# More buffers for the attention units of the first 256 queries, their loads of q and k without the wait for a v, row blocks of layer 1 one step apart, and a new plan

## The chip, the cores and the metric

The kernel runs on one core of a Trainium2 chip. The metric is device time in microseconds (us) from launch to end; of each kernel the median of its runs counts. The core has five instruction queues that matter here: TensorE (PE, matmuls, with its weight loads PEld), VectorE (DVE), ScalarE (ACT), GpSimd (POOL, all but unused) and SyncE (SP, which issues every DMA transfer).

## What is computed

Block-causal attention, an expert layer with softplus, and a second one with SoLU and a normalisation:

```python
# q, k, v: B=4, H=8, S=576, D=64
scores = q @ k.T / sqrt(64)
scores = where(query // 64 >= key // 64, scores, -1e9)
attn = exp(scores - max) / (sum + 1e-9)
x = (attn @ v)                       # -> 2304 tokens x 512
g = log1p(exp(-abs(x @ w_in))) + maximum(x @ w_in, 0)       # 512 -> 2048
x = g @ w_out                                               # 2048 -> 512
h = x @ w_in2                                               # 512 -> 1024
solu = h * softmax(h)
out = ((solu - mean) / sqrt(var + 1e-6) * g_ln) @ w_out2    # 1024 -> 512
```

## The kernel before

**The plan.** The body issues no instruction at once. It adds tasks (a step with its engine, a duration and the tasks it needs) to a `Plan`, whose `run` is a list scheduler: it takes, engine by engine, the ready task of the lowest rank, and writes the instructions out in the order found. A rank is the task's own number plus `RANK[group]` (a base and a slope per member of the group) plus `OFF[step]`. Each engine then works through its own queue strictly in that order. So two tables of numbers set the order on every engine, and a queue whose next instruction has to wait holds up all that stand behind it.

**Attention, first part.** `UnitA` is one of 16 units: one batch element (4) and one pair of heads (4), for the first 256 queries, in fp32. Its steps: SP loads q and k in one tile `qkA` (L515, three buffers) and v in `vA` (L519, two buffers); PE makes the scores with 4 matmuls (`mm_qk`, L204; 8 records in the trace); DVE masks (L538), takes maxima (L543) and scales them (L546); ACT takes exp (L552) into `eA`, one of two fixed tiles; DVE makes reciprocals (L556, L559) and multiplies `eA` by them (`norm`, L564, four instructions); PE transposes `eA` (L571, six); ACT or DVE copies that out of the accumulator into `psA` (one buffer; helper lines L210 on ACT, L212 on DVE); PE multiplies by v (`pv`); ACT or DVE writes the high half of x (L586) and DVE the low half (L590) into `xt`. A unit has its accumulator in the bank R, r, acc or hp. Units 0 to 3 are row block 0 (a row block is 256 tokens), units 4 to 7 row block 1, and so on. `UnitC`, later, does the other 320 queries.

The two loads of a unit depend on each other and on older units so:

```python
self.t_qk = add("SP", ..., self.load_qk, [opened] + g(p1, "t_v") + g(at_of(prev, n - 3), "t_mqk"), DMA_LAT)
self.t_v = add("SP", ..., self.load_v, [opened, self.t_qk] + g(p2, "t_pv"), DMA_LAT)
```

`p1` and `p2` are the unit one and two before; `g(u, "t_v")` is that unit's load of v.

**Weights.** A `Piece` is one 512 KB tile of weights that comes as 64-bit floats and is turned into a high and a low half: SP loads `raw` (L269, three buffers), ACT takes the absolute value (L274), DVE joins bits in three steps (L277, L280, L284, on `a`), ACT or DVE copies the high half, DVE subtracts for the low half (L294). There are 32 such pieces for layer 1, 16 `w1` (w_0 to w_15) and 16 `w2`.

**Layer 1.** A `Pair` is one row block and two of the 16 slices of 128 features: `a` (2 x 24 matmuls with w1 into `hp`, half a pair being 12 here), ACT abs, exp and ln (L647, L650, L653), DVE `stt` (L656), a copy to `gh`, DVE `gl` (L664), then `b` (2 x 12 matmuls with w2 into `acc` for row block 0 and `R` for row block 1). A half pair is thus 12 matmuls of `a` or of `b`. `SEQ` says in which order the pairs come. For the first two row blocks, whose weights are being converted, row block 1 follows row block 0 with the distance `LAG`:

```python
SEQ = [(0, p) for p in range(LAG)]
for p in range(8):
    SEQ += [(1, p)] + ([(0, p + LAG)] if p + LAG < 8 else [])
```

Pair n's `stt` must be done before pair n + 2 writes the same `hp`, and `b` runs in the order of the pairs. Layer 2 (`Tok`, 18 blocks of 128 tokens, with weights `U1` and `U2`) comes last. Four stretches of the span are used below: up to 155 us units, conversions and the first sixteen pairs; to 480 us the later units and row blocks; to 610 us the last row blocks and layer 2's weights; then layer 2.

Of the kernel before, what the change touches and what calls it, by code (L numbers as in the profile page):

```python
# [10 lines left out]
F32 = mybir.dt.float32  # L11
# [10 lines left out]
    "Pair.a": -160.87, "Pair.b": -32.19, "Pair.do_gh": -103.91, "Piece.bits0": 139.36, "Piece.do_lo@P": -201.40,  # L22
    "Piece.do_lo_g": 267.76, "Tok.a": 141.06, "Tok.x_hi": -460.68, "UnitA.x_hi": 408.37, "Tok.tr": -394.45,
    "Tok.bm": 359.77, "UnitC.pv": 348.22, "UnitC.tr": -288.31, "Pair.stt": -191.35, "Pair.do_gl": -445.21,
    "UnitC.qk_lo": -290.12,
}
RANK = {
# [3 lines left out]
    "Tok": (4285.47, -27.327),  # L31
# [163 lines left out]
def body(ctx: ExitStack, tc: tile.TileContext, qk, qkA, vP, vA, w1, w2, u1, u2, gln, out):  # L195
    nc = tc.nc
    PE, ACT, DVE, POOL, SP = nc.tensor, nc.scalar, nc.vector, nc.gpsimd, nc.sync
    plan = Plan()
    XTB, LAG = 3, 2
# [279 lines left out]
    class UnitA:  # L479
# [6 lines left out]
        def plan(self, prev, rank, opened):  # L486
# [11 lines left out]
            self.t_qk = add("SP", dma_ns(262144), rank - 2, self.load_qk, [opened] + g(p1, "t_v") + g(at_of(prev, n - 3), "t_mqk"), DMA_LAT)  # L498
            self.t_v = add("SP", dma_ns(131072), rank - 2, self.load_v, [opened, self.t_qk] + g(p2, "t_pv"), DMA_LAT)
            self.t_mqk = add("PE", 760, rank, self.mm_qk, [self.t_qk] + free)  # L500
            t = chain("DVE", rank, ((200, self.mask), (330, partial(self.max, 0)), (600, partial(self.max, 1)), (70, self.scale)), [self.t_mqk])
            t = add("ACT", 1580, rank, self.exp, [t] + g(p2, "t_tr"))
            t = chain("DVE", rank, ((72, self.den0), (90, self.den1), (918, self.norm)), [t])
            self.t_tr = add("PE", 650, rank, self.tr, [t])
            self.t_cp = add({"ACT": 708, "DVE": 870}, None, rank, self.copy, [self.t_tr] + g(p1, "t_pv"))
# [11 lines left out]
        def load_v(self):  # L517
            self.v = self.t([128, 2, 2, D], "vA")
            SP.dma_start(out=self.v, in_=vA[self.b, self.pr])  # L519

        def mm_qk(self):
# [7 lines left out]
            self.m, self.den = self.t([128, 2, 2], "mA"), self.t([128, 2, 2], "dA")  # L529
# [18 lines left out]
        def exp(self):  # L548
            self.e = state["eA"][self.n % 2]
# [23 lines left out]
        def copy(self, e):  # L573
            self.ps = self.t([128, 2, 384], "psA", 1)
            w = 2 // len(self.st)
            for j, st in enumerate(self.st):
                copy(e, self.ps[:, w * j:w * j + w], st[:, :, 0:384])
# [111 lines left out]
    def open_a():  # L689
# [5 lines left out]
        state["eA"] = [state["pat"].tile([128, 2, 384], F32, name=f"eA{n}") for n in range(2)]  # L695
# [328 lines left out]
```

## Time and profile before

| quantity | value |
|---|---|
| time, median of 3 runs | 810.62 us |
| the runs | 810.79, 810.62, 808.69 us |
| the profiled execution, its own time | 811.79 us |
| span of the profiled execution, first to last instruction | 810.0 us |
| mean granted clock of TensorE in it (1.00 is 2.4 GHz) | 0.989 |
| PE busy | 783.8 us (97%) |
| PEld busy | 694.7 us (86%) |
| DVE busy | 568.3 us (70%) |
| ACT busy | 394.0 us (49%) |
| POOL busy | 0.7 us |

A busy time is the sum of an engine's instructions in the span; PEld overlaps PE. A share is an average over the whole span, so it tells little of a stage; a view of busy time by stretches, views of one engine's waits, and timelines of single instructions stand further down. In a timeline a bracket at the end of a row is idle time just before it, and the instruction whose end closed that idle time.

### The profile page before, as it was taken

To read this page: it belongs to the slowest core of one execution; us is meant where nothing else is said; L and a number is where in the kernel's file an instruction comes from. 1 tells how busy PE (TensorE), PEld (TensorE's weight loads), DVE (VectorE), ACT (ScalarE), POOL (GpSimd) and SP (SyncE) were. 2 spreads that over 40 slices of the span, in tenths; PEclk is the share of its full clock that TensorE was granted. 3 is DMA by queue.
4 is the path that set the end of the run, shared out by engine and by line. 5 is a ranking of instruction groups with operands and counts; after the bars stand their busy time and mean duration, and the time that the engine had idled before them with its cause. 6 is when DMAs were issued, how large, how long until landed. Compare 5 with 4: busy or idle time off the path is not lost.

```text
span 810.0 us, 14410 instructions
## 1 busy us (share of the span) xinstructions
PE 783.8 (97%) x5752; PEld 694.7 (86%) x5752; DVE 568.3 (70%) x1291; ACT 394.0 (49%) x877; POOL 0.7 (0%) x6
## 2 busy tenths in 40 slices
PE   5689999999999999999999999999999999999998
PEld 3478989999888888888888889999898888888887
DVE  6989998565777667667776763768968486766661
ACT  5567776454565455555555553555633232322231
POOL 0000000000000000000000000000000000000000
PEclk9799999999999999999999999999999999999999
DMA  5636542202021112112112200227201111110001
GB/s 179 205 123 190 180 149 77 92 11 79 26 83 41 47 61 67 42 41 68 42 42 57 68 27 27 80 81 249 74 32 43 54 41 42 52 40 27 27 26 53
DMA packets 31203, 59.64 MB, mean 74 GB/s; under 512 B 2849, under 2 KB 14369, under 8 KB 31137
## 3 DMA queue, kind: packets, MB, share of 16 engines
q1 hardware_dynamic: 31136, 58.74, 22.9%
q8 instruction: 45, 0.74, 0.4%
q14 instruction: 22, 0.17, 0.1%
HBM read 49.29 MB, written 9.44 MB: 72 GB/s over the span
## 4 chain that ended last, share of the span: by engine, by line
PE 81%; DVE 8%; DMA 6%; ACT 3%; issue 1%; SPq 0%; ACTq 0%; DVEq 0%
PE hp L204 20%; PE acc L204 18%; PE op L204 12%; PE h L204 11%; PE S L204 5%; PE O L204 5%; PE T L452 4%; DMA raw_u<-in_u_dram 2%; DMA raw<-in_w_dram 2%; PE R L204 2%; PE tp L920 2%; PE r L204 1%; DVE a L284 1%; DVE eA L564 1%; DVE a L280 1%
## 5 line engine op out<-in xcount | busy, mean ns | idle before, releaser
L204 PE MATMUL hp<-xt,w 128*128 128x256 f32 x1728 | 221.6, 284 | 3.7 <-DVE t L656 3.4
L204 PEld LDWEIGHTS hp<-xt,w 128*128 128x128 f32 x1728 | 206.8, 189 | 9.5 <-DVE t L656 5.5
L204 PE MATMUL acc<-gh,w 128*128 128x256 f32 x768 | 148.1, 284 | 0.0
L204 PEld LDWEIGHTS acc<-gh,w 128*128 128x128 f32 x768 | 122.3, 189 | 0.7 <-issue 0.7
L204 PE MATMUL acc<-gl,w 128*128 128x256 f32 x384 | 107.3, 280 | 0.6 <-DVE gl L664 0.6
L204 PE MATMUL op<-w,w2w 128*128 128x512 f32 (+1 forms) x456 | 102.3, 382 | 0.0
L204 PE MATMUL h<-u,w 128*128 128x512 f32 x432 | 101.0, 391 | 0.0
L204 PEld LDWEIGHTS h<-u,w 128*128 128x128 f32 x432 | 80.6, 188 | 16.4
L204 PEld LDWEIGHTS op<-w,w2w 128*128 128x128 f32 x456 | 81.5, 188 | 15.3
L432 ACT ACTIVATE eC<-S,mC 128x384 f32<-128x384 f32 (+2 forms) x80 | 51.8, 649 | 46.4 <-DVE mC L421 46.4
L204 PEld LDWEIGHTS acc<-gl,w 128*128 128x128 f32 x384 | 72.5, 189 | 0.9 <-DVE gl L664 0.8
L656 DVE SCALAR_TENSOR_TENSOR t<-hp,t 128x512 f32<-128x512 f32 x72 | 49.4, 686 | 24.8 <-ACT t L653 24.2
L210 ACT ACTIVATE ps<-T 128x512 f32<-128x512 f32 (+1 forms) x74 | 40.8, 551 | 51.7 <-PE T L452 50.1
L647 ACT ACTIVATE t<-hp 128x512 f32<-128x512 f32 x72 | 42.8, 594 | 34.8 <-DVE gl L664 19.4
L664 DVE TENSOR_TENSOR gl<-t,gh 128x512 fp32r<-128x512 f32 x72 | 49.6, 690 | 3.8 <-ACT gh L210 2.4
L204 PE MATMUL acc<-gh,w2w 128*128 128x256 f32 x256 | 49.8, 285 | 0.0
L417 DVE TENSOR_REDUCE mC<-S 128x2 f32<-128x768 f32 (+2 forms) x48 | 46.9, 976 | 1.5 <-PE S L204 0.4
L650 ACT ACTIVATE t<-t 128x512 f32<-128x512 f32 x72 | 45.5, 633 | 1.8
L653 ACT ACTIVATE t<-t 128x512 f32<-128x512 f32 x72 | 45.2, 628 | 1.3
L452 PE MATMUL T<-ident,eC 128*128 128x128 f32 x288 | 45.3, 275 | 0.0
L872 ACT ACTIVATE e<-h,mx 128x1024 f32<-128x1024 f32 x18 | 20.1, 1116 | 50.5 <-PE tp L920 48.6
L926 ACT ACTIVATE w2w<-tp 128x512 fp32r<-128x512 f32 x36 | 20.7, 596 | 46.2 <-PE op L204 41.4
(156 smaller groups left out, 1128.6 us busy)
## 6 DMA issues: line engine op xcount, KB each, us to landing
raw<-in_w_dram SPq DMA_DIRECT2D x32, 512.0 KB, 4.0
qkC<-in_qk_dram SPq DMA_DIRECT2D x16, 480.0 KB, 3.4
raw_u<-in_u_dram SPq DMA_DIRECT2D x11, 512.0 KB, 3.6
v<-in_vP_dram SPq DMA_DIRECT2D x16, 320.0 KB, 2.9
x2s<-stg SPq DMA_DIRECT2D x18, 256.0 KB, 2.1
xr<-x2s SPq DMA_DIRECT2D x18, 256.0 KB, 3.2
qkA<-in_qkA_dram SPq DMA_DIRECT2D x16, 256.0 KB, 3.4
out_dram<-ob SPq DMA_DIRECT2D x15, 256.0 KB, 2.0
```

What stands on the lines that cost most here:

```text
L204: PE.matmul(out, lhsT, rhs, start=start, stop=stop, skip_group_check=True)
L210: ACT.activation(out, a, AF.Copy)
L417: DVE.tensor_reduce(out=self.m[:, 0:n], in_=self.scores(i), axis=AX.X if i < 2 else AX.XY, op=ALU.max, negate=True)
L432: ACT.activation(e, sc, AF.Exp, scale=0.125, bias=m[:, j:j + 1], accum_out=den[:, j:j + 1])
L452: PE.transpose(T[:, 128 * k:128 * k + 128], e[:, 128 * k:128 * k + 128], ident)
L647: ACT.activation(self.t, self.hp, AF.Abs)
L650: ACT.activation(self.t, self.t, AF.Exp, scale=-1.0)
L653: ACT.activation(self.t, self.t, AF.Ln, bias=1.0)
L656: DVE.scalar_tensor_tensor(out=self.t, in0=self.hp, scalar=0.0, in1=self.t, op0=ALU.max, op1=ALU.add)
L664: DVE.tensor_sub(self.gl, self.t, self.gh)
L872: ACT.activation(self.e, self.hh, AF.Exp, bias=self.mx, accum_out=self.ss)
L926: ACT.activation(self.lh[:, 4 * g:4 * g + 4, :], self.tp[g], AF.Copy)
```

## The change

Five edits and a new plan. `load_qk` of a unit needs the load of q and k before it, no longer the load of v before it. `vA`, `mA` and `dA` have four buffers in place of two, `psA` two in place of one, and `eA` is one of four tiles in place of two; the dependencies follow (a v needs the p*v of the unit four before, an exp the transposes of the unit four before, a copy the p*v two before). `LAG` is 1 in place of 2. The tables `OFF` and `RANK` have new numbers, and six steps that had no offset have one. The scratch space for dynamic DMA is set to 4096. Row numbers in the changed kernel are one or two higher.

```diff
 OFF = {
-    "Pair.a": -160.87, "Pair.b": -32.19, "Pair.do_gh": -103.91, "Piece.bits0": 139.36, "Piece.do_lo@P": -201.40,
...
+    "Pair.a": -75.59, "Pair.b": 18.34, "Pair.do_gh": 35.44, "Piece.bits0": 156.91, "Piece.do_lo@P": -117.94,
...
 RANK = {
-    "first": (278.93, 20.397), "A0": (636.85, 83.080), "A1": (-4008.02, 57.487), "A2": (-200.66, 24.018),
...
+    "first": (278.93, 20.397), "A0": (-2733.73, 86.246), "A1": (-2328.74, -30.508), "A2": (-843.36, 31.422),
...
-    XTB, LAG = 3, 2
+    XTB, LAG = 3, 1
...
-            self.t_qk = add("SP", dma_ns(262144), rank - 2, self.load_qk, [opened] + g(p1, "t_v") + g(at_of(prev, n - 3), "t_mqk"), DMA_LAT)
-            self.t_v = add("SP", dma_ns(131072), rank - 2, self.load_v, [opened, self.t_qk] + g(p2, "t_pv"), DMA_LAT)
+            p4 = at_of(prev, n - 4)
+            self.t_qk = add("SP", dma_ns(262144), rank - 2, self.load_qk, [opened] + g(p1, "t_qk") + g(at_of(prev, n - 3), "t_mqk"), DMA_LAT)
+            self.t_v = add("SP", dma_ns(131072), rank - 1, self.load_v, [opened, self.t_qk] + g(p1, "t_v") + g(p4, "t_pv"), DMA_LAT)
...
-            t = add("ACT", 1580, rank, self.exp, [t] + g(p2, "t_tr"))
+            t = add("ACT", 1580, rank, self.exp, [t] + g(p4, "t_tr"))
...
-            self.t_cp = add({"ACT": 708, "DVE": 870}, None, rank, self.copy, [self.t_tr] + g(p1, "t_pv"))
+            self.t_cp = add({"ACT": 708, "DVE": 870}, None, rank, self.copy, [self.t_tr] + g(p2, "t_pv"))
...
-            self.v = self.t([128, 2, 2, D], "vA")
+            self.v = self.t([128, 2, 2, D], "vA", 4)
...
-            self.m, self.den = self.t([128, 2, 2], "mA"), self.t([128, 2, 2], "dA")
+            self.m, self.den = self.t([128, 2, 2], "mA", 4), self.t([128, 2, 2], "dA", 4)
...
-            self.e = state["eA"][self.n % 2]
+            self.e = state["eA"][self.n % 4]
...
-            self.ps = self.t([128, 2, 384], "psA", 1)
+            self.ps = self.t([128, 2, 384], "psA", 2)
...
-        state["eA"] = [state["pat"].tile([128, 2, 384], F32, name=f"eA{n}") for n in range(2)]
+        state["eA"] = [state["pat"].tile([128, 2, 384], F32, name=f"eA{n}") for n in range(4)]
...
-    nc = _bacc.Bacc("TRN2", target_bir_lowering=False, num_devices=1)
+    nc = _bacc.Bacc("TRN2", target_bir_lowering=False, num_devices=1, dynamic_dma_scratch_size=4096)
```

The order moves on every engine. Three places follow, of before and then of the changed kernel.

The DMA queue (SP) at the start of the program, before; the numbers name the buffers, and the qkA loads are those of units 0 to 3 in order:

```order
L515 DMA qkA_136<-in_qkA_dram 128x512
L519 DMA vA_138<-in_vA_dram 128x256
L515 DMA qkA_140<-in_qkA_dram 128x512
L519 DMA vA_142<-in_vA_dram 128x256
L515 DMA qkA_144<-in_qkA_dram 128x512
L269 DMA raw_152<-in_w1_dram 128x1024
L269 DMA raw_162<-in_w1_dram 128x1024
L269 DMA raw_179<-in_w2_dram 128x1024
L519 DMA vA_237<-in_vA_dram 128x256
L515 DMA qkA_245<-in_qkA_dram 128x512
L269 DMA raw_253<-in_w1_dram 128x1024
```

The q and k of unit 3 (qkA_245) stand behind three weight pieces and the v of unit 2.

The same queue in the changed kernel:

```order
L517 DMA qkA_138<-in_qkA_dram 128x512
L521 DMA vA_140<-in_vA_dram 128x256
L517 DMA qkA_142<-in_qkA_dram 128x512
L521 DMA vA_144<-in_vA_dram 128x256
L517 DMA qkA_146<-in_qkA_dram 128x512
L521 DMA vA_154<-in_vA_dram 128x256
L270 DMA raw_156<-in_w1_dram 128x1024
L517 DMA qkA_167<-in_qkA_dram 128x512
L521 DMA vA_182<-in_vA_dram 128x256
L517 DMA qkA_185<-in_qkA_dram 128x512
L517 DMA qkA_190<-in_qkA_dram 128x512
L270 DMA raw_197<-in_w1_dram 128x1024
```

Unit 3's q and k (qkA_167) now stand behind one weight piece; the second weight piece has moved behind the q and k of unit 5, and four loads of v stand in front of it.

DVE, from the normalisation of unit 1 on (it multiplies eA_131), before:

```order
L564 TENSOR_SCALAR eA_131<-eA_131,dA 128x128 x2
L564 TENSOR_SCALAR eA_131<-eA_131,dA 128x256 x2
L277 TENSOR_SCALAR a<-a 128x512 x2
L280 SCALAR_TENSOR_TENSOR a<-raw,a 128x512 x2
L284 SCALAR_TENSOR_TENSOR a<-raw,a 128x512 x2
L556 TENSOR_SCALAR dA<-dA 128x4
L212 CAST xt<-R 128x256
L559 RECIPROCAL dA<-dA 128x4
L212 CAST w_0_81<-a 128x512
L590 TENSOR_TENSOR xt<-R,xt 128x256
L564 TENSOR_SCALAR eA_130<-eA_130,dA 128x128 x2
L564 TENSOR_SCALAR eA_130<-eA_130,dA 128x256 x2
```

Two weight pieces and the x of unit 0 stand between the normalisations of units 1 and 2 (unit 2 uses eA_130 again).

The same place in the changed kernel:

```order
L566 TENSOR_SCALAR eA_131<-eA_131,dA 128x128 x2
L566 TENSOR_SCALAR eA_131<-eA_131,dA 128x256 x2
L558 TENSOR_SCALAR dA<-dA 128x4
L545 TENSOR_REDUCE mA<-hp_114 128x1
L545 TENSOR_REDUCE mA<-hp_115 128x1
L561 RECIPROCAL dA<-dA 128x4
L278 TENSOR_SCALAR a<-a 128x512
L548 TENSOR_SCALAR mA<-mA 128x4
L566 TENSOR_SCALAR eA_132<-eA_132,dA 128x128 x2
L566 TENSOR_SCALAR eA_132<-eA_132,dA 128x256 x2
```

Unit 2's normalisation (eA_132, a tile of its own) comes six instructions behind unit 1's, and unit 3's maxima (hp) stand among them; the first weight piece has one of its three steps there.

PE behind the first `b` (w_0_97 and w_1_98 are the first two w2 tiles, acc belongs to row block 0), before:

```order
L204 MATMUL acc<-gh,w_1_98 128x256
L571 MATMUL r<-ident,eA_130 128x128 x6
L204 MATMUL r<-psA,vA 64x256 x2
L204 MATMUL r<-psA,vA 64x128 x2
L571 MATMUL R<-ident,eA_131 128x128 x6
L204 MATMUL acc<-gh,w_2_99 128x256
```

Behind the last matmul of the first b stand the transposes and p*v of unit 6 and the transposes of unit 7, then the second b of row block 0.

The same place in the changed kernel:

```order
L205 MATMUL acc<-gh,w_1_98 128x256
L205 MATMUL hp_115<-xt,w_0_81 128x256 x12
L205 MATMUL hp_115<-xt,w_1_82 128x256 x12
L205 MATMUL hp_114<-xt,w_2_83 128x256 x12
L205 MATMUL hp_114<-xt,w_3_84 128x256 x12
L205 MATMUL r<-qkA 128x128 x2
L205 MATMUL r<-qkA 128x256 x2
L205 MATMUL hp_115<-xt,w_2_83 128x256 x12
L205 MATMUL hp_115<-xt,w_3_84 128x256 x12
L205 MATMUL R<-gh,w_0_97 128x256
```

The units 6 and 7 are now ahead of the first b. Behind it stand four half pairs (row block 1 on w_0 and w_1, row block 0 on w_2 and w_3), the scores of a later unit, two more half pairs, and then the first b of row block 1 (into R).

## Rows read from the trace of the kernel before

**Rows 1.** Busy us by stretch: length, PE, PEld, DVE, ACT, POOL, clock, DMA share, GB/s.

```profile
0.00:40.00 40.00, 23.62 (x137) 16.23 (x138) 33.06 (x101) 22.86 (x69) 0.70 (x6) 0.83 0.58 194
40.00:70.00 30.00, 26.40 (x214) 22.88 (x214) 27.53 (x69) 21.55 (x54) 0.00 (x0) 0.94 0.48 147
70.00:155.00 85.00, 83.67 (x716) 79.09 (x717) 75.01 (x162) 55.18 (x116) 0.00 (x0) 1.00 0.42 134
155.00:480.00 325.00, 325.00 (x2709) 288.32 (x2708) 221.29 (x527) 175.66 (x411) 0.00 (x0) 1.00 0.17 51
480.00:610.00 130.00, 128.31 (x1025) 123.02 (x1025) 86.88 (x168) 60.47 (x106) 0.00 (x0) 1.00 0.28 90
```

**Rows 2.** Waits of PE, 0 to 71 us: us in total, times, longest.

```profile
PE R L204 <- DMA qkA<-in_qkA_dram: 7.7, 2, 4.2
PE r L204 <- ACT psA L210: 3.6, 2, 2.1
...
PE r L204 <- DVE psA L212: 2.2, 1, 2.2
```

**Rows 3.** SP's waits, 0 to 120 us; its timeline (start, duration), unit 3's load.

```profile
SPq L519 <- PE R L204: 20.0, 3, 11.1
...
16.06 0.43 SPq L515 DMA_DIRECT2D qkA<-in_qkA_dram  x1
```

**Rows 4.** PE timeline (start, duration, instruction, count): one row for each kind of step.

```profile
18.91 0.93 PE L204 MATMUL hp<-qkA 64*128 64x128 f32 x8
...
27.07 1.65 PE L204 MATMUL R<-qkA 64*128 64x128 f32 x8 [4.16 <-DMA qkA<-in_qkA_dram]
...
57.45 0.93 PE L204 MATMUL r<-qkA 64*128 64x128 f32 x8
58.30 0.87 PE L204 MATMUL R<-psA,vA 128*64 128x256 f32 x8
...
76.05 5.60 PE L204 MATMUL hp<-xt,w 128*128 128x256 f32 x48
...
86.93 0.82 PE L571 MATMUL r<-ident,eA 128*128 128x128 f32 x6
```

**Rows 5.** PE timeline: the first and the 15th b, gaps between them.

```profile
46.88 0.39 PE L204 MATMUL acc<-gh,w 128*128 128x256 f32 x1
...
52.89 1.55 PE L204 MATMUL r<-psA,vA 128*64 128x256 f32 x8 [2.08 <-ACT psA L210]
...
68.31 1.64 PE L204 MATMUL hp<-xt,w 128*128 128x256 f32 x12 [1.47 <-DVE t L656]
...
114.75 0.39 PE L204 MATMUL acc<-gl,w 128*128 128x256 f32 x1 [0.58 <-DVE gl L664]
...
147.15 0.28 PE L204 MATMUL R<-gh,w2w 128*128 128x256 f32 x1
```

**Rows 6.** DVE timeline: masks, norms, bit steps, the first and the 13th gl.

```profile
7.42 0.27 DVE L538 MEMSET r<- 64x256 f32 x1 [0.77 <-PE r L204]
...
10.96 1.01 DVE L564 TENSOR_SCALAR eA<-eA,dA 128x128 f32<-128x128 f32 x4
...
13.21 0.76 DVE L277 TENSOR_SCALAR a<-a 128x512 int32<-128x512 int32 x2
13.88 1.29 DVE L280 SCALAR_TENSOR_TENSOR a<-raw,a 128x512 int32<-128x512 int32 x2
...
42.48 0.27 DVE L538 MEMSET r<- 64x256 f32 x1 [1.21 <-PE r L204]
...
45.52 0.67 DVE L664 TENSOR_TENSOR gl<-t,gh 128x512 fp32r<-128x512 f32 x1
...
130.26 0.68 DVE L664 TENSOR_TENSOR gl<-t,gh 128x512 fp32r<-128x512 f32 x1
```

**Rows 7.** ACT timeline: abs and ln of the first pair.

```profile
47.23 0.61 ACT L647 ACTIVATE t<-hp 128x512 f32<-128x512 f32 x1
...
48.54 0.64 ACT L653 ACTIVATE t<-t 128x512 f32<-128x512 f32 x1
```

More of the change, by code (lines that the diff above doesn't have):

```diff
@@ L21 @@
 OFF = {
-    "Pair.a": -160.87, "Pair.b": -32.19, "Pair.do_gh": -103.91, "Piece.bits0": 139.36, "Piece.do_lo@P": -201.40,
-    "Piece.do_lo_g": 267.76, "Tok.a": 141.06, "Tok.x_hi": -460.68, "UnitA.x_hi": 408.37, "Tok.tr": -394.45,
-    "Tok.bm": 359.77, "UnitC.pv": 348.22, "UnitC.tr": -288.31, "Pair.stt": -191.35, "Pair.do_gl": -445.21,
-    "UnitC.qk_lo": -290.12,
+    "Pair.a": -75.59, "Pair.b": 18.34, "Pair.do_gh": 35.44, "Piece.bits0": 156.91, "Piece.do_lo@P": -117.94,
+    "Piece.do_lo_g": 39.95, "Tok.a": 311.98, "Tok.x_hi": -596.65, "UnitA.x_hi": 667.22, "Tok.tr": -141.11,
+    "Tok.bm": 453.62, "UnitC.pv": 162.36, "UnitC.tr": -166.97, "Pair.stt": -175.92, "Pair.do_gl": -199.23,
+    "UnitC.qk_lo": -536.59, "Piece.do_hi": -94.45, "UnitA.copy": 176.03, "UnitA.exp": 182.87,
+    "UnitA.norm": 173.41, "Piece.abs": 751.71, "Piece.load": -87.26,
 }
 RANK = {
[3 rows of a table removed]
-    "Tok": (4285.47, -27.327),
[3 rows of a table added]
+    "Tok": (4184.20, -7.771),
 }
```

4 rows, old and new, of the table RANK are left out of this document.

## The prediction, made before the changed kernel ran

> **What bounds the kernel now.** I read the busy time by stage first [rows 1]. TensorE (PE) is the engine that sets the end: it works without a gap from 155 to 480 us. Its idle time lies at the front: 40.0 - 23.6 = 16.4 us of the first 40 us, 3.6 us from 40 to 70, 1.3 us from 70 to 155, then 1.7 us from 480 to 610. At the front its granted clock is low too, 0.83 and 0.94. In the same front the other full engine is VectorE (DVE): 27.5 of 30 us and 75.0 of 85 us, against 221 of 325 us later. So the front is a race of two queues, and only there can this change win anything; matmuls are neither added nor taken away.
>
> Next the waits of PE [rows 2]: 7.7 us for two loads of q and k, 5.8 us for the copies of psA by ScalarE and DVE. The waits of the DMA queue [rows 3] say why q and k are late: SP stands 11.1 us at the most before a load of v, since v has two buffers and the third load needs unit 0's last matmul. The q and k of unit 3 stand behind that load and go at 16.06 us.
>
> Then a count. I add up PE's work in the order of its instructions at full clock: a score step 0.87 us, a transpose step 0.65, a p*v step 0.82, half a pair of layer 1 1.39 (a) or 1.38 (b); these are the distances to the next start, a little under the durations of [rows 4], where 48 matmuls of a are four halves. What a start is later than the work ahead of it I call the **lag**; it holds idle time, the slow clock and the joins between steps. Ahead of the first b of pair (0,0) stand 8 score, 6 transpose, 6 p*v steps and 4 half pairs, 21.3 us; it starts at 46.88, a lag of 25.5 us. Ahead of the 15th b (fifteen of the first sixteen pairs) stand 13 score, 12 transpose, 12 p*v steps and 60 half pairs, 112.1 us; it starts at 147.15, a lag of 35.1 us. Of the 9.5 us in between, 4.7 are idle (2.08, 1.47 and two of nearly 0.6 us), 1.7 are the slow clock behind the first of these gaps (p*v, transpose and half a pair from 52.89 to 57.45 took 4.56 us where 2.85 would do), and 3.1 us are the joins [rows 5]. From there on the PE queue is saturated, so the lag at the 15th b is the number to forecast.
>
> **The change part by part.**
>
> *Loads.* The same 16 loads of q and k, 16 of v, 32 of weights, one queue. The load of unit 3's q and k now needs only unit 0's score matmuls, done at 5.2 us, and not v; it can go at some 5.4 us in place of 16.06. At its own 2.8 us to landing (16.06 to the matmul at 18.91 [rows 3, 4]) it is there by 8.5 us, as soon as PE is done with unit 2's scores. What is queued behind it: v, two more q and k, one weight piece; the second and third weight pieces move back from 3 to 4 us to about 9 and 11 us. They land 4 us later at 13 to 15 us; DVE's order, by the sums below, wants the first piece at 13.8 and the second at 20 us. Cost nothing; the cover is the eight units' attention on DVE. The new wait of a v for the unit four before it holds up weight loads behind it; by then three pieces are ahead (three raw buffers, as before).
>
> *Buffers of mA, dA, eA, psA.* They take away a DVE wait (the third maximum stood until unit 0's exp had read its own) and let units 0 to 3 run abreast: the norm of unit 2 follows that of unit 1 after 6 short instructions, not 11 longer ones. DVE's own work does not shrink. Up to the first gl DVE now has two more units: 32 norm instructions for 24, 18 maxima for 16, 24 small ones for 19. By the spacings of [rows 6] (0.60 us for a two-operand step on 512 columns, 0.34 for a one-operand one, 0.92 for four norms) the sum up to and with it is 37.5 us before and 40.3 us after. Before, that gl ended at 45.52 + 0.60 = 46.1 us: 5.3 us start, 37.5 work, 2.5 idle (three waits, the first 0.77 and the longest 1.21) and 0.8 that my spacings miss. After: 5.3 + 40.3 + 0.77 + 0.85 = 47.3 us, and PE's b starts at about 47.6. **So the early loads do not bring the first b forward; it comes 0.7 us later.** But ahead of it PE has 8 whole units and only two half pairs, 21.5 us, so the lag is 26.1, and units 6 and 7 no longer stand behind it.
>
> *One step apart (LAG 1).* Behind the first b, before, stand the transposes and p*v of unit 6, which wait for psA: the 2.08 us gap and the slow clock behind it. Now four half pairs stand there (row block 1 on the same weights, then the next weights), whose inputs are ready: x of units 6 and 7 at some 50.3 us by DVE's order, the b ending at 50.4. The 4.7 us of gaps and the 1.7 us of slow clock are thus open to gain, 6.4 us. The price of LAG 1 is on DVE: the stt of pair (1,0) stands where DVE comes to it at about 54.3 us, while PE ends that a at some 53.7 and ScalarE's abs, exp and ln take 1.95 us more (47.23 to 49.18 [rows 7]); DVE stands some 1.4 us there. For the later pairs my queue sums give 1 to 3 us of slack.
>
> *Where the queues meet again.* The tightest place is the 13th b (weights 12 and 13 of block 0). DVE's sum to the 13th gl is 117.9 us before, 117.3 after. Before, it ended at 130.26 + 0.61 = 130.9 us [rows 6]: 5.3 start, 4.6 idle (nine waits), 3.1 missed by the spacings. After, with 0.77 + 1.4 + some 0.7 idle: 5.3 + 117.3 + 2.9 + 3.1 = 128.6 us. PE's work ahead is 98.65 us; lag 26.1, 0.7 us for a p*v step that still runs slow just before the first b, 2.6 of joins, so PE comes at 128.05: it waits 0.5 us. Bounds: DVE idle of 0.77 us alone gives no wait; DVE idle as now (4.6) plus the 1.4 gives 131.7, a wait of 3.6 us. I take the middle count because each of its terms has a row.
>
> *The new plan elsewhere.* From 155 to 480 us the new order has per unit the same three score steps, six transposes and two pairs in another sequence; PE idle there is zero now, so it cannot gain, and DVE at 68% leaves room: zero, up to 1 us worse. From 480 to 610 us DVE's order now has the last eight gl ahead of most of the second matrix's conversion, so PE's 1.7 us of idle time there [rows 1] may go: zero taken, down to -1.7. The smaller scratch for dynamic DMA buys the space for the buffers; all transfers are issued by SP and none by POOL in the profile; zero, and no row prices it (up to 1 us).
>
> **Sum.** Lag at the 15th b: 26.1 + 0.7 + 3.1 + 0.5 = 30.4 us, start at 142.5 in place of 147.15; the work ahead is the same 112.1 us. Gain 4.6 us. The profiled execution took 811.79 us for a span of 810.0; 807.2 us by its own measure. It lies 1.2 us above the median 810.62 of the runs, from which I go: **806.0 us**. Low end: no wait, no slow step, and the 1.7 us at 480 to 610 gone, -7.5: 803.1. High end of this case: the wait of 3.6 us, -1.5: 809.1.
>
> **Rivals.**
>
> *A colder front.* Before the first b the units now come in two blocks of four, and PE, by the same sums, stands idle some 4.6 us twice (22 to 26.7 and 37 to 41.8 us). The trace shows what follows such a gap: a score step took 1.65 us behind the 4.16 us wait at 27.07, and 0.93 at 18.91 [rows 4]. If the clock stays at 1.2 GHz from 26.7 to beyond the first b, about 7 us of work takes 14; 4.8 us of that falls into the second gap, so b starts 2.2 us later and its own first half is slow, 0.7: gain 1.7 us, 808.9. The Trainium skill, TensorE: Matmul & The Clock Gate, "Loop structure matters more than you think", says matmuls kept back to back stay fast and a long wait before each makes PE cold; by that rule LAG 1 is right behind the first b and the two blocks of units are wrong before it, and the time would be this rival's.
>
> *DVE in lockstep (slower).* One queue in order: a stt that comes before its ln holds up weights and norms behind it. With LAG 1 both row blocks use the same weights, so PE's a, ScalarE's chain and DVE's stt follow each other more closely. If DVE stands not 1.4 us once but 1 us at each of the 12 pairs up to the 13th b, its gl comes 10.6 us later, at 139 us, PE waits 11 us, and the time is 6 us above now: 816.5. It turns to a loss from about 0.45 us per pair. For it: DVE has no room here [rows 1], and the first stt does wait. Against it: the later a's end 3 to 8 us before their stt by my sums.
>
> *Gain given back.* The front gains, and the rearranged later stages, where PE has no gap now, open 3 us or more of them (0.2 us in each of 16 units): 809 to 811. Likewise if the change doesn't do what it says: loads early, but DVE bound all the same with its idle time as now: 809.1.
>
> **How the numbers follow.** A measurement of this kernel tells about 0.3% (2.4 us) from no change. Forecast 0.64; colder front 0.11; given back 0.13; lockstep 0.12. Faster by over 0.3% (below 808.2): the forecast but for its upper end, and a little of the given back, 0.65. Within: 0.23. Slower: 0.12. The range goes from 803.0 to 810.5 us, which leaves out the lockstep and some of the given back.
>
> **What would show it.** Unit 3's score matmuls at 9 to 10 us, not 18.9; SP's longest wait for v below 5 us; the first b at 47 to 49 us, not earlier; no PE gap over 1 us from 50 to 120 us; the 15th b at 142 to 144 us; a DVE wait of 1 to 2 us at 54 us before a stt. Wrong if the first b comes well before 46 us (then DVE's sum isn't what binds) or if PE waits for gl or t by several us between 60 and 150.

## The result, and the profile after

| | before | changed |
|---|---|---|
| time, median, first comparison | 809.65 us (4 runs) | 800.11 us (799.71 to 801.25, 4 runs) |
| changed over before, 95% interval | | 0.9876 (0.9857 to 0.9894) |
| the same, two later comparisons | | 0.9898 (0.9878 to 0.9918), 0.9887 (0.9866 to 0.9908) |
| profiled execution, its own time | 811.79 us | 799.75 us |
| span | 810.0 us | 798.0 us |
| PE, DVE, ACT busy | 783.8, 568.3, 394.0 us | 777.8, 561.1, 406.2 us |

The change gains 1.0 to 1.2%, 8 to 10 us; 4.6 us was forecast, and 800.1 us lies below the range of 803.0 to 810.5. The two profiled executions differ by 12.0 us, which is too much: the one of before lies above its median and the one of the changed kernel below its own. A second profile of before (809.86 us) and two more of the changed kernel (803.06 and 802.92 us) set that right below.

The changed kernel by stage, to be read against [rows 1] (stretch, length, busy us of PE, PEld, DVE, ACT, POOL, clock, DMA share, GB/s):

```profile
0.00:40.00 40.00, 25.26 (x172) 17.41 (x172) 33.66 (x106) 25.98 (x84) 0.70 (x6) 0.87 0.64 211
40.00:70.00 30.00, 28.30 (x221) 25.65 (x222) 28.03 (x67) 22.48 (x48) 0.00 (x0) 0.89 0.46 150
70.00:155.00 85.00, 84.66 (x733) 79.76 (x732) 76.46 (x174) 53.67 (x118) 0.00 (x0) 1.00 0.41 134
155.00:480.00 325.00, 325.00 (x2714) 289.83 (x2713) 217.43 (x538) 185.74 (x396) 0.00 (x0) 1.00 0.16 50
480.00:610.00 130.00, 129.80 (x1019) 123.69 (x1018) 91.98 (x165) 65.63 (x114) 0.00 (x0) 1.00 0.28 90
```

PE's idle time falls in every stretch that had some: 14.7 for 16.4 us, 1.7 for 3.6, 0.3 for 1.3, 0.2 for 1.7. Its matmul count in the first 40 us goes from 137 to 172. VectorE (DVE) is as full as before, and the clock from 40 to 70 us is lower (0.89 for 0.94): neither explains the gain.

PE's timeline of the changed kernel (start, duration, instruction, idle time before it), the places that the prediction named:

```profile
8.89 0.93 PE L205 MATMUL hp<-qkA 64*128 64x128 f32 x8 [1.11 <-DMA qkA<-in_qkA_dram]
...
25.92 1.70 PE L573 MATMUL R<-ident,eA 128*128 128x128 f32 x6 [4.78 <-DVE eA L566]
...
41.10 1.70 PE L573 MATMUL R<-ident,eA 128*128 128x128 f32 x6 [4.66 <-ACT eA L554]
...
47.74 0.52 PE L205 MATMUL acc<-gh,w 128*128 128x256 f32 x1
...
50.72 5.60 PE L205 MATMUL hp<-xt,w 128*128 128x256 f32 x48
...
126.28 0.39 PE L205 MATMUL acc<-gl,w2w 128*128 128x256 f32 x1 [0.33 <-DVE gl L666]
...
140.10 0.28 PE L205 MATMUL acc<-gh,w2w 128*128 128x256 f32 x1
```

Unit 3's scores start at 8.89 us (18.91 before), two gaps of nearly 5 us follow, the first b starts at 47.74 (46.88), and four half pairs follow it at full clock without a gap (50.72, 48 matmuls in 5.60 us) where before PE waited 2.08 us for psA [rows 5]. The 15th b starts at 140.10 us (147.15). (The 48 matmuls are four half pairs of 12: the `a` of a pair is 2 x 12 matmuls, not the 2 x 24 that the description of the kernel says.)

**One measure for all runs.** Each matmul record counts with the median distance to the next record of its kind from 60 us on (0.114 us for one of layer 1); all 5752 sum to 736.4 us in either kernel. What a start is later than the count ahead of it is the lag, as in the prediction, only with finer prices (a score step 0.65 for 0.87), so that some 18.5 us of work stand ahead of the first b. "To 438" and "to 560" are what the lag grows up to so much work, about the end of the second attention part and the end of layer 1:

| profile of | first b at | lag there | to the 15th b | 15th b at | to 438 | to 560 |
|---|---|---|---|---|---|---|
| before | 46.88 | 28.4 | +12.6 | 147.15 | +23.8 | +4.9 |
| before, second | 47.81 | 29.3 | +10.9 | 146.42 | +23.8 | +3.7 |
| changed | 47.74 | 29.3 | +4.5 | 140.10 | +23.0 | +0.8 |
| changed, second | 48.88 | 30.5 | +5.2 | 141.94 | +23.0 | +2.3 |
| changed, third | 48.40 | 30.0 | +5.6 | 141.80 | +23.3 | +2.0 |

By the means of these rows, two and three executions, the change loses 1.1 us up to the first b, gains 6.6 us from there to the 15th, 0.8 us up to 438 and 2.7 us up to 560: 9.0 us, as the times say. The front is thus 5.5 us of it, and 3.5 us lie in stages that were taken as zero.

### The profile page after: what moved, and what is told of

It is laid out like the page before. It is cut to its first block, busy times and chain, and to the rows that moved or that the text cites. A ratio compares the mean times of both kernels' runs of the same rounds, so it can differ in the third digit from the quotient of the medians.

```text
span 798.0 us, 14451 instructions
## 1 busy us (share of the span) xinstructions
PE 777.8 (97%) x5752; PEld 691.3 (87%) x5752; DVE 561.1 (70%) x1299; ACT 406.2 (51%) x869; POOL 0.7 (0%) x6
## 4 chain that ended last, share of the span: by engine, by line
PE 79%; DVE 14%; ACT 2%; DMA 2%; issue 2%; SPq 0%; DVEq 0%; ACTq 0%
PE hp L205 18%; PE acc L205 18%; PE op L205 12%; PE h L205 12%; PE S L205 5%; PE O L205 5%; PE T L453 4%; PE tp L922 2%; DVE a L285 2%; DVE a L281 2%; DVE t L658 1%; DMA e<-in_u_dram 1%; PE R L205 1%; DVE w L295 1%; DVE gl L666 1%
## 5 line engine op out<-in xcount | busy, mean ns | idle before, releaser
L205 PE MATMUL hp<-xt,w 128*128 128x256 f32 x1728 | 217.9, 280 | 0.0
L211 ACT ACTIVATE ps<-T 128x512 f32<-128x512 f32 (+1 forms) x55 | 30.7, 559 | 23.3 <-PE T L453 23.2
```

The costliest lines, as they stand in the source:

```text
L205: PE.matmul(out, lhsT, rhs, start=start, stop=stop, skip_group_check=True)
L211: ACT.activation(out, a, AF.Copy)
```

## The experiments

### The two stages, taken apart

The plan's list of tasks was cut at the last p*v of the second attention part (about 500 us). One kernel runs the changed list up to the cut and the list of before from it on, the other the reverse:

```diff
-for t in order: self.emit(t)
+for t in listed(changed plan up to the last UnitC.pv, then the rest in the order before): self.emit(t)
```

> The changed kernel up to the last p*v of the second attention part, from there on the order of the plan before on every engine. Theory (two separate gains: 7 to 8 us in the front, by lag, and some 4 us between 480 and 600 us): 4 us slower than the changed kernel, so 5.5 us faster than before; PE waits for t (stt) again six or seven times between 490 and 570 us, some 3 us by the weight loads' wait. Rival (one gain in the front, the later difference follows from PE coming early): as fast as the changed kernel, 9.5 us faster than before, no such waits.

> The kernel before up to the last p*v of the second attention part, from there on the changed plan's order. Theory (two separate gains): 4 us faster than before, 805.5 us; no PE wait over 0.4 us behind 490 us; the 15th b at 147 us as before. Rival (the later stage gains only because of the front): 0 us.

Measured: front new 804.27 us, 0.9927 (0.9910 to 0.9945); tail new 808.52 us, 0.9977 (0.9964 to 0.9990). Gains of 5.9 and 1.9 us. Both stages gain by themselves; the rival that one follows from the other falls. (Up to 438 the lag grows by 23.1 us with the new front and by 23.8 with the old one, so the 0.8 us go with the order up to the cut.) The later stage alone brought less than the 4 us expected, by the times; in its trace the lag grows by 1.5 us up to 560 where before has 3.7 to 4.9, so 2.2 to 3.4. The waits of the weight loads (PEld; us, times, longest) behind 480 us tell them apart. Before, 480 to 615 us:

```profile
PEld hp L204 <- DVE t L656: 2.9, 6, 1.2
```

The changed kernel, same stretch:

```profile
PEld acc L205 <- DVE gl L666: 0.4, 1, 0.4
```

(In its second and third profile two waits for gl make 1.5 and 1.2 us; none is for t.)

Front new and tail old, 480 to 620 us:

```profile
PEld hp L323 <- DVE t L776: 2.6, 5, 0.8
```

Front old and tail new, 480 to 620 us:

```profile
PEld acc L322 <- DVE gl L782: 0.5, 1, 0.5
```

The five or six waits for t, the stt of an older pair that still holds the hp buffer, go in these four kernels with the old order of this stage, whatever the front. In PE's own waits of before only two of them show (same stretch):

```profile
PE hp L204 <- DVE t L656: 1.4, 2, 1.0
```

In the records the starts show seven: a distance to the next matmul of 0.18 to 1.24 us where 0.114 is usual, each followed by a second one of 0.22. They make 3.5 of the 4.9 us. The order of PE tells where they come from: the list of before runs two a, then two b (a74 a75 b71 b72 a76 a77 b73 b74; a74 is the a of row block 7, pair 4), the changed one alternates (a74 b72 a75 b73 a76 b74).

To put the blame on that alternation, PE alone got the old order behind the cut:

```diff
 PE, behind the cut:
-a74 b72 a75 b73 a76 b74 a77 b75
+a74 a75 b71 b72 a76 a77 b73 b74
```

> The changed kernel; only PE's own order behind the last p*v of the second attention part is that of the plan before (two a in a row, then two b); ScalarE, VectorE and SP keep the changed order there. Theory that PE's alternation of a and b is what gains in that stage (two hp buffers, so a third a in a row waits for a stt): 3 to 4 us slower than the changed kernel, waits of hp for t back at five or more places. Rival that VectorE's order (stt and gl ahead of the conversion of the second matrix) is what gains: within 1 us of the changed kernel.

Measured: 861.65 us, 1.0636 (1.0599 to 1.0673). Neither theory had that: 60 us are lost, since the other engines stand in the changed order and each waits for the other's older pair. PE's costliest wait, 470 to 760 us:

```profile
PE hp L323 <- DVE t L776: 31.5, 9, 7.2
```

And DVE's, same stretch:

```profile
DVE gh L331 <- PE acc L323: 45.5, 9, 9.2
```

So the alternation alone isn't shown as the cause; what is shown is that the order of this stage on all engines together takes the waits for t away, and what queues out of step cost here: 31.5 us of idle time at nine places, up to 7.2 us each, for this one wait. Three kernels of the next sections speak against the alternation as the whole cause: the changed one with LAG 2, plan_noise_b, and before with the new tables. PE alternates there too (a70 a71 a72 b70 a73 b71 a74, where the changed kernel has a70 a71 a72 a73 b70 b71 a74), and still the lag grows by 6.0, 4.6 and 4.6 us from 438 to 560. By the weight loads PE waits for t 1.8, 0.8 and 0.6 us from 490 to 640 us, and for gl 1.9 us in each.

> The kernel before, a second profile. The first profiled execution took 811.79 us, 1.2 to 2.1 us over the median. Theory that executions differ in the front (when the first loads land and what clock PE gets up to 60 us): a shorter execution has the 15th b 1 to 2 us earlier than 147.15 us and the same spans behind it. Rival that they differ in the later stages: the 15th b at 147.0 to 147.3 us whatever the time.

The second execution of before (809.86 us) has its 15th b at 146.42, 0.7 us earlier, and loses 1.2 us less in the later stage; from the 15th b to 438 both lose 23.8. Both theories hold in part: executions differ in the front and at the later waits. Of the 1.7 us by which the two differ from the first to the 15th b, 1.2 are the clock: behind the same wait of 2.08 us for psA, the steps up to the next score step took 4.56 us in the first profile and 3.37 in the second, with a granted clock of 0.68 (in part at 1.2 GHz) and 1.00 (2.4 GHz) from 53 to 58 us.

### Parts of the change alone

```diff
 before_lag1:         XTB, LAG = 3, 1                       (the rest as before)
 after_lag2:          XTB, LAG = 3, 2                       (the rest as changed)
 buffers_loads_only:  changed kernel, LAG = 2, OFF and RANK of before
 after_old_loads:     changed kernel, t_qk waits for p1.t_v, vA with 2 buffers, t_v as before
```

> The kernel before with LAG 1 alone; loads, buffers and tables as before. Its DVE queue up to the first gl is as long as before (37.3 us of steps), and the units 6 and 7 stand behind the first b on PE as before. Theory (LAG 1 fills the queue behind the first b only if the units 6 and 7 are ahead of it, since its half pairs need their x): the 2 us wait for psA behind the first b stays, the 15th b at 146 to 148 us, 809 to 811 us. Rival (LAG 1 by itself takes away the gaps): 15th b at 140 to 143 us, 804 to 806 us.

> The changed kernel with LAG 2 alone. The order that follows has the first gl behind the same 40.0 us of DVE steps, 23.5 us of PE's work ahead of the first b, unit 6's p*v behind its first half. Theory (what gains is that the units are ahead of the first b, LAG 1 matters little): first b at 47.5 to 48.5 us, 15th b at 139 to 141 us, within 1 us of the changed kernel, 800 to 801 us. Rival (LAG 1 is what gains): 15th b at 145 to 147 us, 805 to 807 us.

> The kernel before with the buffers and the loads of the changed one, LAG 2 and the old tables. First gl behind 33.6 us of DVE steps and 18.6 us of PE's work. Theory (VectorE's queue sets the first b, then the 13th gl): first b at 41 to 43 us; DVE's sum to the 13th gl is 118.6 us, with 9.3 us on top as in the changed kernel 127.9, so PE, with 102.1 us of work ahead of that b, cannot be further than a lag of 25.8: 15th b at 139.5 to 142 us; the waits for t behind 500 us as before; 803 to 805.5 us. Rival (the buffers pay only with LAG 1): 15th b at 146 to 148 us, 809 to 811 us.

> The changed kernel with the loads as before: a q and k waits for the v before it, two buffers of v. The order that follows has the q and k of unit 3 behind three weight pieces again, 41.5 us of DVE steps ahead of the first gl and the units 6 and 7 behind the first b. Theory (the early loads do not feed PE as such; they decide which units come ahead of the first b): unit 3's scores at 18 to 20 us, first b at 48.5 to 50.5 us with only 19.2 us of work ahead of it, a wait of 1 to 3 us behind it, 15th b at 144 to 147 us, 803 to 806.5 us. Rival (the loads are hidden by VectorE's queue anyway): 15th b at 140 to 141.5 us, 800 to 801.5 us.

| kernel | time | over before | first b at | to the 15th b | 15th b at |
|---|---|---|---|---|---|
| LAG 1 alone | 816.31 | 1.0067 (1.0042 to 1.0092) | 46.35 | +15.7 | 152.52 |
| changed, LAG 2 | 812.91 | 1.0027 (1.0013 to 1.0041) | 48.52 | +12.6 | 147.55 |
| buffers and loads | 809.73 | 0.9992 (0.9975 to 1.0008) | 41.59 | +14.2 | 146.21 |
| changed, old loads | 813.87 | 1.0026 (1.0008 to 1.0044) | 51.01 | +15.4 | 156.22 |

No part gains by itself (buffers and loads were tried only together), and LAG 1 or the loads taken from the changed kernel cost the whole gain and more. My sums gave the first b within 0.5 us (47.5 to 48.5, 41 to 43 and 48.5 to 50.5 us were expected in the last three rows) but not the 15th: LAG 1 alone was expected at 146 to 148, LAG 2 at 139 to 141, buffers and loads at 139.5 to 142, old loads at 144 to 147. All four times lie above what was expected, by 5, 12, 4 and 7 us; of the rivals only that of buffers and loads holds. Buffers and loads show it best: the first b 5 to 6 us earlier, and all of that given back. That kernel from 40 to 110 us, columns as in the first view:

```profile
40.00:110.00 70.00, 64.69 (x537) 60.66 (x538) 69.32 (x159) 49.02 (x109) 0.00 (x0) 0.98 0.51 166
```

Its PE waits, 41 to 147 us:

```profile
PE acc L204 <- DVE mA L547: 3.5, 1, 3.5
PE r L204 <- ACT psA L210: 1.9, 1, 1.9
PE r L204 <- DVE xt L591: 1.5, 1, 1.5
```

DVE is busy 69.3 of 70 us: b starts early, and PE waits later, for what DVE has not done yet (3.5 us for mA, 1.5 for xt). In the changed kernel with LAG 2 PE waits for weights and for norms, which with LAG 1 it does not in the same stretch (PE's waits, 48 to 156 us):

```profile
PE r L573 <- DVE eA L566: 3.0, 3, 1.6
PE hp L205 <- DVE w L295: 2.2, 2, 1.3
```

With LAG 2, row block 0 runs ahead into weights that DVE has not converted; that is a reading of these two rows, not a test.

### Is it the part, or the order that comes with it?

Each of those kernels is also a new order by the scheduler, with numbers meant for another case. Two kernels keep every part and change an assumption of the scheduler only; two exchange the tables:

```diff
 plan_noise_a:  DMA_LAT = 1700.0 -> 1750.0
 plan_noise_b:  MARGIN "PE": 600.0 -> 620.0
 after_old_tables, before_new_tables:  OFF and RANK of the other kernel
```

> The changed kernel; only the scheduler's assumed landing time of a DMA is 1750 in place of 1700 ns, which changes nothing but the order it finds. Up to the first b the units stand as in the changed kernel; DVE's sum to the 13th gl is 113.6 us (116.9 in the changed kernel), PE's work there the same 98.6. Theory (what gains is which units stand ahead of the first b and how much DVE work ahead of each gl): first b at 47.5 to 49 us, 15th b at 139.5 to 142 us, 799.5 to 802 us. Rival (the tables fit one order only, any other loses as the LAG 2 order did): 805 us or more.

> The changed kernel; only the scheduler's margin for PE tasks is 620 in place of 600 ns. In the order that follows unit 6's p*v stands behind the first b, DVE's sum to the 13th gl is 120.1 us and PE's work ahead of the 13th b 101.4. Theory (as for the other disturbed plan): DVE reaches the 13th gl 9 to 13 us behind its sum, at 129.5 to 133 us, a wait or two behind the first b, 15th b at 143 to 145.5 us, 803 to 805.5 us. Rival (any other order loses the whole gain): 15th b at 146 to 148 us, 808 to 813 us. Other rival (nothing depends on the order in detail): 800 to 801.5 us.

> The changed kernel with the tables of before: LAG 1, the buffers and the loads are kept. First gl behind 33.6 us of DVE steps, the units 6 and 7 behind the first b, 124.1 us of DVE steps ahead of the 13th gl and 105.7 us of PE's work ahead of the 13th b. Theory (order, not parts): first b at 41 to 43 us and yet the 15th b only at 144 to 148 us, waits for t behind 500 us, 807 to 811 us. Rival (the three parts bring the front's gain with any tables): 15th b at 140 to 142 us, 803 to 805 us.

> The kernel before with the new tables alone: LAG 2, old loads and buffers. 42.4 us of DVE steps ahead of the first gl, 22.0 us of PE's work ahead of the first b, unit 6's p*v and unit 7 behind it. Theory (order and parts go together): first b at 49 to 52 us, 15th b at 146 to 150 us, no waits for t behind 500 us, 806 to 810 us. Rival (the tables bring the gain without the parts): 15th b at 141 to 144 us, 800 to 804 us.

| kernel | time | over before | first b at | to the 15th b | 15th b at |
|---|---|---|---|---|---|
| plan_noise_a | 803.13 | 0.9913 (0.9893 to 0.9933) | 48.79 | +5.5 | 142.15 |
| plan_noise_b | 812.13 | 1.0022 (1.0008 to 1.0036) | 49.56 | +9.8 | 147.84 |
| changed, old tables | 810.17 | 1.0000 (0.9985 to 1.0015) | 40.34 | +15.4 | 146.20 |
| before, new tables | 813.91 | 1.0045 (1.0022 to 1.0069) | 52.24 | +10.8 | 150.06 |

20 ns in one assumption lose all of the gain, with every part of the change in place. So the single results above are no prices of LAG 1, of loads or of buffers: they are prices of orders. Of the four expectations only that for the old tables holds in time and 15th b (the first b came 0.7 us early); plan_noise_a came 1.1 us above its range, before with the new tables 3.9 above, and plan_noise_b, put at 803 to 805.5 us, lost the gain as its rival said. So my sums of steps did not foretell what an order costs. What the gaining orders (changed, plan_noise_a) share, and none of the others so far has, is that units 0 to 7 are done on PE ahead of the first b, and row block 1 follows at once. In plan_noise_b unit 6's p*v stands behind the first b; its timeline between 45 and 57 us:

```profile
45.93 1.55 PE L205 MATMUL R<-psA,vA 128*64 128x256 f32 x8 [1.68 <-DVE psA L213]
48.22 1.69 PE L573 MATMUL r<-ident,eA 128*128 128x128 f32 x6 [0.74 <-DVE eA L566]
...
53.61 0.87 PE L205 MATMUL r<-psA,vA 128*64 128x256 f32 x8
...
56.06 2.21 PE L205 MATMUL hp<-xt,w 128*128 128x256 f32 x17 [0.56 <-DVE xt L592]
```

The row at 53.61 is that p*v, and the wait at 56.06 is for its x: 0.56 us. Further on this order waits 1.4 us for t and 1.3 us for psA as well. To see whether the place costs by itself, one step was moved in the changed list, and the changed kernel ran beside it (tr7 is the transposes of unit 7, pv6 the p*v of unit 6, b00 a half of the first b, a10 the a of row block 1, pair 0):

```diff
 PE:
-tr7 tr6 pv7 pv6 b00 b00 a10
+tr7 tr6 pv7 b00 b00 pv6 a10
```

> The changed kernel's order, with one step moved: unit 6's p*v (8 matmuls in the records, 0.8 us) stands behind the first b on PE in place of ahead of it; all other engines keep their order. Theory (a unit behind the first b costs by itself): the b still waits for its gl, so it starts at most 0.7 us earlier; x of unit 6 is then 3 us later, PE waits 1 to 2 us for it before the first a of row block 1, VectorE stands 2 to 3 us at unit 6's low half; 15th b 1.5 to 3 us later than the 140.1 and 141.9 us of the changed kernel, time 1.5 to 3 us over it. Rival (the order as a whole, this place does not matter): 15th b and time within 0.7 us of the changed kernel.

> The changed kernel beside it, on the same chip, a third profile: 799.7 to 803 us, 15th b between 140 and 142 us.

Measured: 803.34 us, 0.9898 (0.9875 to 0.9922), beside 802.55 us, 0.9887 (0.9866 to 0.9908). The 15th b starts at 144.04 us, 2.2 us later than beside it (141.80), as the theory said; VectorE stands behind the late x (its waits, 45 to 60 us):

```profile
DVE xt L710 <- ACT xt L329: 3.2, 1, 3.2
```

PE's own waits behind it are small, 0.4 us for psA, 0.4 for xt and 0.3 for t (45 to 141 us), and not the 1 to 2 us expected ahead of the first a of row block 1. About 1 us of the 2.2 is the clock in the first b: from 48 to 51 us the granted clock was 0.51 (nearly all at 1.2 GHz), beside it 0.85, and 0.53 and 0.99 in the second and first profile of the changed kernel. Up to 560, 1.2 us come back (+0.8 for +2.0), and the two times differ by 0.8 us, where the theory had 1.5 to 3 and which is less than their intervals tell apart. So the gain of the whole does not need this place; in the front it costs 1 to 2 of the 6.6 us, by one pair of profiles.

### VectorE's load

```diff
         def bits1(self):
-            DVE.scalar_tensor_tensor(out=self.a, in0=self.raw[:, :, 1], scalar=-0x80000000, in1=self.a, ...)
+            pass
```

> The changed kernel without the second of three bit steps on VectorE in each of the 48 weight pieces (the sign is left out of the weights), same order of all else. Eight such steps of 0.60 us stand on VectorE ahead of the first gl, 32 ahead of the 15th. Theory (VectorE's queue sets the first b and what follows): first b 3 to 4.8 us earlier, at 43 to 44.7 us, 15th b at 136 to 138 us, 796 to 798 us. Rival (PE's chain of units and the loads set it): first b at 46.5 to 48 us, time within 1 us of the changed kernel.

> The kernel before with the same step left out (signs left out of the weights), eight of them ahead of its first gl too. Theory (behind the first b it is PE's order that costs: units 6 and 7 stand there and wait for their copies, whatever VectorE's sum is): first b at 42 to 44 us, the waits behind it stay at 2 to 4 us, 15th b at 142 to 145 us, 805 to 808 us. Rival (both kernels differ only by VectorE's load ahead of each gl): with 19 us less on VectorE the front's difference is gone, 15th b at 136 to 139 us, some 4 us behind the changed kernel without the step, for the later stage.

Measured: changed 798.00 us, 0.9850 (0.9826 to 0.9873); before 805.14 us, 0.9933 (0.9909 to 0.9957). 3.6 us come off the changed kernel (801.63 us beside it), 4.7 off before. First b at 46.58 and 44.67 us: 1.2 to 2.3 us and 2.2 to 3.1 us earlier, not the 3 to 4.8 that eight steps of 0.60 make. In the changed kernel PE then stands before the transposes all the same (its waits, 20 to 140 us):

```profile
PE R L572 <- DVE eA L565: 8.3, 2, 4.7
PE r L572 <- DVE eA L565: 1.4, 1, 1.4
```

The norms are VectorE's own instructions, so this wait alone doesn't tell its queue from the chain ahead of them. But from 5 to 47 us VectorE is now busy 37.9 us, 39.8 to 40.7 with the step, and waits 1.1 us in three for exp, 0.4 at most with it. So VectorE's queue sets the first b only for the first 1 to 2 us of relief; behind that the chain of scores, maxima, exp and norm sets it, at nearly the same time. Behind the first b before needs 8.8 us without the step (10.9 to 12.6 with it), the changed kernel 4.6 (4.5 to 5.6): the changed order no longer depends on VectorE's load there, the order before does with 2 us (4 against its first profile, with the slow clock), and 4 us remain, which are waits for psA, t and gl (2.3, 1.0 and 0.5 us by the distances between starts). The expectation of 142 to 145 us for the 15th b of before was missed (141.14), the rival's 136 to 139 as well: both causes count. The wait for psA behind the first b is there as before (PE's waits, 44 to 142 us):

```profile
PE r L204 <- ACT psA L210: 2.1, 1, 2.1
```

A version that might beat both moves four copies to ScalarE in the changed list:

```diff
-Piece.do_hi (2), UnitA.x_hi (unit 4), Pair.do_gh (0,0): DVE
+the same four, same places: ACT
```

> The changed kernel's order, with four copies of the first 47 us (two high halves of weights, one of x, the first gh) on ScalarE in place of VectorE, at the same places: 4 x 0.34 = 1.4 us less on VectorE ahead of the first gl, 2.2 us more on ScalarE. Theory (VectorE sets the first b): first b 0.8 to 1.3 us earlier than in the changed kernel, and 0.5 to 1.3 us off the time. Rival (ScalarE's exps come later by what is put ahead of them and PE's transposes with them): first b not earlier, time same or up to 1.5 us more.

> The changed kernel again, on the chip of the other three, with a second profile. If the first profile is typical: first b at 47 to 48.5 us, 15th b at 139.5 to 141 us, no PE wait over 0.5 us from 50 to 590 us, 799.5 to 801.5 us. If it was a lucky execution: 1 to 2 us later at the first b.

802.35 us, 0.9903 (0.9883 to 0.9924), beside 801.63 us, 0.9898: no gain. The first b at 49.16 us is not earlier (48.88 beside it), and PE waits 10.3 us for norms in the first 160 us, 9.3 us beside it:

```profile
PE R L691 <- DVE eA L684: 10.3, 3, 5.6
```

That agrees with the chain, and not VectorE's sum, being next. The second profile of the changed kernel, 803.06 us with waits of up to 0.8 us for gl behind 580 us, also says that its first one was a lucky execution.

## Why the prediction was wrong, step by step

**Right, with sizes.** The loads: unit 3's q and k go at 5.22 us (5.4 forecast) and its scores start at 8.89, 9.92 and 9.31 us in the three profiles (9 to 10), SP's longest wait for a v is 4.1 us (under 5):

```profile
SPq L521 <- PE R L205: 8.2, 3, 4.1
...
5.22 0.33 SPq L517 DMA_DIRECT2D qkA<-in_qkA_dram  x1
```

(SP's waits from 0 to 120 us, and its timeline.) The first b isn't earlier: 47.74, 48.88 and 48.40 us, 47.6 forecast. The two gaps ahead of it, 4.78 and 4.66 us, were put at some 4.6 us each. LAG 1's price on VectorE is there, 1.79 us at 55.60 us (1.4 at 54.3 forecast; 2.54 and 2.09 us in the other two profiles), behind the gl that feeds the first b (DVE's timeline):

```profile
46.33 0.67 DVE L666 TENSOR_TENSOR gl<-t,gh 128x512 fp32r<-128x512 f32 x1
...
55.60 0.69 DVE L658 SCALAR_TENSOR_TENSOR t<-hp,t 128x512 f32<-128x512 f32 x1 [1.79 <-ACT t L655]
```

The 13th b waits 0.33 us for its gl (0.5 forecast). No PE gap is over 1 us between 50 and 120 us.

**The front's size.** The 15th b was put at 142.5 us; it starts at 140.10, 141.94 and 141.80, and before at 147.15 and 146.42. The front's gain is 4.5 to 7.0 us by single pairs, 5.5 by the means, for 4.6. The term that was too dear is the 3.1 us of joins between steps, taken over unchanged. In the prediction's prices the changed kernel's first profile has 28.0 us of lag at the 15th b and 26.2 at the first, 1.8 us for 4.3 (2.5 and 2.8 in the other two profiles): 0.33 idle, some 0.25 of slow clock, and 1.2 us of joins. The rest of the 3.1 us belonged to the waits and went with them: in the distances between starts the gaps of 2.08, 1.47 and 0.58 us [rows 5] are 2.25, 1.63 and 0.83 us, a fourth is 0.70 for 0.54, and four more of 0.19 to 0.31 us, with 0 to 0.14 us of idle time each, were not in my count; together 1.7 us. In the other direction, the 1.7 us of slow clock held 0.5 us of joins: the same steps at full clock took 3.37 us in the second profile of before, not 2.85.

**The step that failed** is the new plan elsewhere: from 155 to 480 us "PE idle there is zero now, so it cannot gain" and from 480 to 610 us "zero taken, down to -1.7". The first is wrong by 0.8 us (23.8 for 23.0 to 23.3 of lag): 325.00 us busy of 325 hid joins between steps, which an order can have fewer of. No distance between starts there is over 0.22 us longer than usual in any of the five profiles, so no wait is hidden in it; those that are over 0.06 us longer number 405 in both profiles of before and 392 or 393 in those of the changed kernel. The Trainium skill, Perfetto Trace Analysis, "Identifying the Most-Contended Engine", says that matmul busy time tells badly how far PE is from its limit, and names instead the share of the peak rate that the matmuls reach and the weight loads' busy share; this case agrees, with PE at 325.00 us in both profiles and PEld at 288.32 before and 289.83 now. The second is wrong by 2.7 us (1.5 to 4.1 by single pairs): I bounded the gain by PE's idle time of 1.7 us, where the waits for t held 3.5 us by the distances and 2.9 by the weight loads, and I looked at VectorE's order there and not at PE's a and b. With 0.8 and 2.7 us in place of zero, and the front as forecast, the sum would have been 802.5 us.

**The rivals.** The colder front: the clock did fall behind the two gaps (transposes of 1.70 us at 25.92 and 41.10 where the one of [rows 4] took 0.82), and the lag at the first b is 1.1 us up, but b did not come 2.2 us later. In all three profiles it starts 0.74 us behind the end of its gl (47.00, 48.14 and 47.66 us), when the p*v of unit 6, at the slow clock and without idle time before it, is done (PE's timeline):

```profile
46.32 1.49 PE L205 MATMUL r<-psA,vA 128*64 128x256 f32 x8
```

At full clock that step takes 0.87 us [rows 4], so the slow clock costs about 0.6 us just there: the 0.7 us that the sum had for it. The lockstep on VectorE did not occur, neither in the changed order nor in those near it that lost the gain: from 48 to 140 us VectorE waits 1.8 us for its ln in the changed kernel (once), 1.2 in plan_noise_b and 1.8 with LAG 2 (three times each), not 1 us at each pair. The gain was not given back later; more was added.

**Left open.** Which edit or place of the order takes away what between the first and the 15th b. The distances show what went: before, PE waits there for psA (2.25 us in both profiles, with 1.2 us of slow clock behind it in one), for t (1.63 and 0.70 us; 1.67 and 0.37 in the second) and for gl (0.83 in both), and a few times under 0.35 us; the changed kernel waits only for the 13th gl (0.4 to 0.5). Also open are which joins make the 0.8 us, and what besides the alternation of a and b the later stage needs, since no order of the other engines was found here that fits the old one of PE. A price of the smaller scratch space was not measured by itself.

## What to carry to other kernels

Where in-order queues are tied by two buffers, an order is one thing: price a new order on every stage, and look for runs of the same kind of step (a, a, b, b) that need more buffers than there are (here the waits for t went with such runs, but three orders without them lost as much). Read PE's losses from the distances between matmul starts or from the weight loads' waits, not from its idle time alone, and don't take a stage without idle time for one that can't gain. A part of a change that is planned anew can't be priced by running it alone: disturb the planner first, and see how much the disturbance costs.

## What the runs showed that I had not expected

PE's idle time in the profile understates its waits: 1.4 us in two waits by the matmuls, 2.9 us in six by the weight loads, 3.5 us in seven by the distances, all for the same DVE step from 480 to 615 us. The Trainium skill, Perfetto Trace Analysis, "Tensor Engine Instruction (MATMUL, LD_WEIGHTS)", says that the end of a matmul in the trace is modelled; these three numbers agree. Executions of one kernel differ by 1.9 us in span (before: 810.0 and 808.1) and by 3.3 us (changed: 798.0, 801.1 and 801.3), at three places only: up to the first b, from there to the 15th, and at the later waits.
